# Linear attention and a token and channel mixer: transposes by DMA instead of TensorE

## The chip, the cores and the metric

The kernel runs on one core of a Trainium2 chip. The metric is the device time of one execution in microseconds (us); less is better. A core has TensorE (PE), VectorE (DVE), ScalarE (ACT), GpSimd (POOL) and SyncE (SP), each with its own in-order stream of instructions, and 16 DMA engines that all queues share.

## What is computed

Eight batches, eight heads, 576 tokens, head size 64. The attention's output, heads side by side, is x with 512 columns; the mixer works on it.

```python
q_p, k_p = phi(q), phi(k)            # phi(x) = (x if x > 0 else exp(x) - 1) + 1
kv  = einsum('bhsd,bhse->bhde', k_p, v)
z   = sum(k_p, axis=2)
num = einsum('bhsd,bhde->bhse', q_p, kv)
den = einsum('bhsd,bhd->bhs', q_p, z)[..., None] + 1e-06
x   = (num / den) as [8, 576, 512]
u   = x + (relu(x^T @ w_tok1) @ w_tok2)^T     # w_tok1 576x256, w_tok2 256x576
out = u + relu(u @ w_ch1) @ w_ch2             # w_ch1 512x1536, w_ch2 1536x512
```

Inputs and output are float32 in HBM; the matmuls take bf16 and add up in float32.

## The kernel before

**Tokens.** The first 512 tokens of a batch lie four to a partition (R = 4: token 4p + r is on partition p); the last 64, the tail, lie on one half of the partitions, the lower half for even batches and the upper for odd ones, as a fifth piece r = 4. The tails of a pair of batches share one tile, `ut`, so that the channel part works on pairs: 4 + 4 + 1 tiles of 128 tokens.

**Steps for one batch**, by helper and line. `load` (L98) issues on SP, for one half g of the heads, a 512 KB DMA (L103) and the tail's 64 KB (L107; q's tail goes to both halves of the partitions, two DMAs). `phi` (L137) makes k' into `kp` or q' into `qp`: exp on ACT (L117), +1, min and max on DVE (L123, L131, L132). `vcast` (L142) casts v, with a column of ones per head, so that z comes out of the kv matmul. `kv` (L154): 40 matmuls of 64 columns of weights and 65 moving columns, two heads side by side in the array, copied by ACT into `kvd`, the two heads of a pair on the two halves of the partitions. `qtr` (L181): 20 TensorE transposes of q', copied by ACT (L187) into `qT`. `nd` (L217): 40 matmuls with a contraction of 64, then DVE adds EPS, inverts and multiplies into `x` (L206 to L211), in five pieces. `mm1` (L224) and `mm2` (L237), the token mixer: ten and eight matmuls of 512 columns, relu on ACT (L235), the residual add into `u` on DVE (L245); `mm2_tail` (L248) does the tails of a pair together, in half-width matmuls. `utr` (L258): 16 transposes of u, copied by ACT and DVE into `uT`; `utr_tail` (L330) four for the tails, into `uTt`. `mm3` (L340): four matmuls of 512 columns into one of twelve channel tiles, relu on ACT into `cr` (L350); `mm3_tail` (L352) 16 matmuls of 128 columns. `mm4` (L363): twelve matmuls of 512 columns for one tile of tokens, in three parts, the residual add (L379) and the store (L383), issued on POOL, for the last pair on SP.

**Order.** It is written out by hand. After a start in which batch 0 goes through in small pieces, `run` (L523) takes a list of big steps, `mm3` and `mm4`, and puts small ones behind them at given numbers: "step 10" is what stands behind the eleventh big step. During the big steps of batch n, called stage n in the prediction, the small steps of batch n + 1 run (kv to u), and phi for batch n + 2 (`prep_k` and `prep_q`, L389 and L396), which also issue the loads of the batch after that in the same buffers. An even stage has 24 big steps (12 `mm3`, 12 `mm4`), an odd one 30 (12, 3 of the tail, 15). The numbers are in `at0`, `at1` and `AT` (L554, L573, L583); stage 0 and 1 have lists of their own. Of small steps with one number the one earlier in the list goes first; every engine and the SP queue sees its part of the program in this order. `raw`, `qT`, `x`, `u` and `uT` exist twice, by the parity of the batch; `kp`, `qp`, `vs` and `uTt` once. PSUM has four banks for the big steps and two tiles of two banks, tag "sm", which all small steps take in turn.

**Loads.** Batch 0's are issued first, then the weights; batch 1's, 2's (L504) and 3's (L569) stand between the start and stage 1; from batch 4 on they are issued by `prep_k` and `prep_q` of the batch two earlier.

Of the kernel before, what the change touches and what calls it, by code (L numbers as in the profile page):

```python
# [18 lines left out]
def kernel(  # L19
# [44 lines left out]
    w1t = const("w1t", [128, 128])  # L64
    w2 = const("w2", [128, NT, S])
    wc1 = const("wc1", [128, NDM, DCH])
# [8 lines left out]
    qT = [const(f"qT{b}", [128, HP, R1, 128]) for b in range(2)]  # L75
    kvd = [const(f"kvd{b}", [128, HP, D1]) for b in range(2)]
# [4 lines left out]
    uT = [const(f"uT{b}", [128, NDM, R, 128]) for b in range(2)]  # L81
# [16 lines left out]
    def load(nm, n, g, gate=None):  # L98
        b = n % 2
        hs = slice(HG * g, HG * g + HG)  # L100
        dst = raw[nm, b]
        s = src[nm][n, hs, 0:SM, :].rearrange("h (p r) d -> p h r d", r=R)
        ins = after(nc.sync.dma_start(out=dst[:, hs, 0:R, :].rearrange("p h r d -> p h (r d)"),  # L103
                                      in_=s.rearrange("p h r d -> p h (r d)")), gate)
        for i in range(2):
            if nm == "q" or i == b:
                nc.sync.dma_start(out=dst[half[i], hs, R, :],  # L107
                                  in_=src[nm][n, hs, SM:S, :].transpose([1, 0, 2]))
        return ins
# [44 lines left out]
    def kv(n, g, first=False):  # L154
        b = n % 2
        if first:
            ps = bank()
        else:
            ps = ps_sm.tile([128, 2, 512], FP32, name="kv_ps", tag="sm")[:, 0]
        ps = ps[:, 0:2 * D1].rearrange("p (j e) -> p j e", j=2)  # L160
        for i in range(2):
            for r in range(R1):
                for a in range(2):
                    h = 2 * (2 * g + i) + a
                    nc.tensor.matmul(out=ps[half[a], i], lhsT=kp[:, r, h, :],
                                     rhs=(vst[b] if r == R else vs[:, r])[:, h, :],
                                     start=(r == 0), stop=(r == R))
        nc.scalar.copy(out=kvd[b][:, 2 * g:2 * g + 2], in_=ps)

    def qtr_pair(n, j, tp, put):  # L170
# [5 lines left out]
        if put == "act":  # L176
            nc.scalar.copy(out=qT[b][:, j], in_=tp[:, 0:R1])
        elif put == "dve":
            nc.vector.tensor_copy(out=qT[b][:, j], in_=tp[:, 0:R1])

    def qtr(n, g):  # L181
# [3 lines left out]
        for i in range(2):  # L185
            qtr_pair(n, 2 * g + i, tp[:, i * R1:(i + 1) * R1], None)
        nc.scalar.copy(out=qT[b][:, 2 * g:2 * g + 2].rearrange("p j r c -> p (j r) c"),  # L187
                       in_=tp[:, 0:2 * R1])

    def nd_mm(n, rs, j0, nj):  # L190
        b = n % 2
        ps = ps_sm.tile([128, 2, 512], FP32, name="nd_ps", tag="sm")
        for i, r in enumerate(rs):
            for j in range(nj):
                at = D1 * (nj * i + j)
                for a in range(2):
                    nc.tensor.matmul(out=ps[:, a, at:at + D1], lhsT=qT[b][half[a], j0 + j, r, :],  # L197
                                     rhs=kvd[b][half[a], j0 + j, :], start=True, stop=True)
        live["nd", j0, rs[0]] = ps

    def nd_end(n, rs, j0, nj):
        b = n % 2
        m = nj * len(rs)
        v_ = live["nd", j0, rs[0]][:, :, 0:m * D1].rearrange("p a (i e) -> p a i e", i=m)
        den = work.tile([128, 2, 4], FP32, name="den", tag="den")[:, :, 0:m]
        nc.vector.tensor_scalar(out=den, in0=v_[:, :, :, D:D1].rearrange("p a i o -> p a (i o)"),  # L206
                                scalar1=EPS, scalar2=None, op0=ALU.add)
        nc.vector.reciprocal(out=den, in_=den)  # L208
        for i, r in enumerate(rs):
            js = slice(nj * i, nj * i + nj)  # L210
            nc.vector.tensor_tensor(  # L211
                out=x[b][:, r, 2 * D * j0:2 * D * (j0 + nj)].rearrange(
                    "p (j a d) -> p a j d", j=nj, a=2),
                in0=v_[:, :, js, 0:D],
                in1=den[:, :, js, None].to_broadcast([128, 2, nj, D]), op=ALU.mult)

    def nd(n, r):  # L217
        nd_mm(n, [r], 0, HP)
        nd_end(n, [r], 0, HP)
# [4 lines left out]
    def mm1(n):  # L224
        b = n % 2
        ps = ps_sm.tile([128, NT, DM], FP32, name="a_ps", tag="sm")
        for mt in range(NT):
            for r in range(R):
                nc.tensor.matmul(out=ps[:, mt], lhsT=w1[:, r, 128 * mt:128 * mt + 128],  # L229
                                 rhs=x[b][:, r, :], start=(r == 0), stop=False)  # L230
        for mt in range(NT):
            nc.tensor.matmul(out=ps[:, mt], lhsT=w1t[half[mt]], rhs=x[b][half[mt], R, :],  # L232
                             start=False, stop=True)
# [3 lines left out]
    def mm2(n, rs):  # L237
# [3 lines left out]
        for i, r in enumerate(rs):  # L241
            for kt in range(NT):
                nc.tensor.matmul(out=ps[:, i], lhsT=w2v[:, kt, r], rhs=ar[b][:, kt, :],  # L243
                                 start=(kt == 0), stop=(kt == NT - 1))
        nc.vector.tensor_tensor(out=u[b][:, rs[0]:rs[0] + m], in0=ps[:, 0:m],  # L245
                                in1=x[b][:, rs[0]:rs[0] + m], op=ALU.add)

    def mm2_tail(p):  # L248
        ps = ps_sm.tile([128, 2, DM], FP32, name="h_ps", tag="sm")[:, 0]
        for kt in range(NT):  # L250
            for b in range(2):
                nc.tensor.matmul(out=ps[half[b]], lhsT=w2[:, kt, SM:S], rhs=ar[b][:, kt, :],
                                 start=(kt == 0), stop=(kt == NT - 1))
        for b in range(2):
# [369 lines left out]
```

## Time and profile before

| what | us |
|---|---|
| median of three runs | 306.9 |
| the three runs | 306.6, 307.05, 306.9 |
| the profiled execution | 306.6 |
| its span, first to last instruction | 304.8 |
| PE busy | 278.0 (91%) |
| DVE busy | 165.1 (54%) |
| ACT busy | 159.7 (52%) |
| POOL busy | 26.9 (9%) |
| mean granted TensorE clock | 0.993 of full speed |
| DMA | 42.90 MB, a mean of 141 GB/s |

The page comes from one profiled execution. "Busy" is the time in which an engine works on an instruction; TensorE's matmuls overlap each other, their ends are modelled, and so a row's duration is longer than the distance to the next one. The slices cut the span into 40 parts of 7.62 us; a digit is the busy share in tenths. In a timeline each row has start, duration, engine, line, operation, output and inputs, the number of instructions, and in brackets the idle time before it with what ended it. SPq is the SP queue in the act of issuing a DMA.

### The profile page before, as it was taken

The page shows a single profiled execution, that of the slowest core. Times are in us where ns is not written, and L with a number is a line of the kernel's source. Part 1 is how long each engine was busy: PE and PEld are TensorE (multiplying, and loading weights), DVE is VectorE, ACT ScalarE, POOL GpSimd, SP SyncE. Part 2 cuts the span into 40 slices and gives each one's busy share as a digit, 9 for nine tenths or more (in the row PEclk, how much of TensorE's full clock was granted, in tenths as well). Part 3 has the DMA queues.
Part 4 walks back from the last instruction along what each step waited for, and adds up shares of the span by engine and source line. Part 5 has one row for each costly group of instructions (what it writes and reads, how often), then busy time and mean ns, then how long its engine had stood idle before and what let it go on. Part 6 is the DMA issues. An engine that isn't in the chain of part 4 may idle for free.

```text
span 304.8 us, 5592 instructions
## 1 busy us (share of the span) xinstructions
PE 278.0 (91%) x2274; PEld 146.9 (48%) x2312; DVE 165.1 (54%) x309; ACT 159.7 (52%) x236; POOL 26.9 (9%) x49
## 2 busy tenths in 40 slices
PE   8888969977999999899998999899997999999993
PEld 8765434433744544354464454355463454454641
DVE  4793476395487844981658325791738515440021
ACT  3654753149936476457495075656486074226500
POOL 1070020030001100010001200010000210000000
PEclk9999979999999999999999999999999999999999
DMA  6999998999999920973058710011001210010032
GB/s 196 282 144 205 305 242 201 283 296 338 252 291 290 304 82 0 264 242 117 2 160 243 226 30 0 23 66 53 2 0 37 103 37 0 34 71 34 2 96 76
DMA packets 50585, 42.90 MB, mean 141 GB/s; under 512 B 19136, under 2 KB 47552, under 8 KB 50560
## 3 DMA queue, kind: packets, MB, share of 16 engines
q1 hardware_dynamic: 44064, 31.73, 38.0%
q0 software_dynamic: 6496, 10.82, 14.8%
q8 instruction: 18, 0.29, 0.5%
q14 instruction: 7, 0.06, 0.1%
HBM read 36.83 MB, written 9.44 MB: 152 GB/s over the span
## 4 chain that ended last, share of the span: by engine, by line
PE 57%; DMA 12%; ACT 11%; DVE 8%; SPq 5%; issue 4%; POOL 1%; ACTq 0%
PE h_ps L369 24%; PE c_ps L346 19%; DMA q_raw<-in_q_dram 8%; ACT qT L187 5%; PE a_ps L229 4%; DVE u L245 4%; SPq L107 3%; PE nd_ps L197 3%; DMA wc<-in_moe_w_ch_dram 3%; PE c_ps L357 3%; ACT cr L350 3%; SPq L103 2%; ACT e L117 2%; DVE ut L256 2%; PE tp L266 2%
## 5 line engine op out<-in xcount | busy, mean ns | idle before, releaser
L346 PE MATMUL c_ps<-uT,wc 128*128 128x512 bf16 x366 | 92.0, 380 | 3.7 <-ACT cr L350 1.5
L369 PE MATMUL h_ps<-wc,cr 128*128 128x512 bf16 x371 | 90.6, 383 | 2.2 <-ACT cr L350 1.4
L350 ACT ACTIVATE cr<-c_ps 128x512 bf16<-128x512 f32 x96 | 56.5, 599 | 56.3 <-PE c_ps L346 55.6
L369 PEld LDWEIGHTS <-cr 128*128 128x128 bf16 x384 | 36.1, 99 | 44.3 <-issue 3.5
L346 PEld LDWEIGHTS <-wc 128*128 128x128 bf16 x384 | 33.8, 98 | 39.0 <-issue 5.1
L379 DVE TENSOR_TENSOR o_sb<-h_ps,u 128x512 f32<-128x512 f32 x32 | 21.8, 686 | 20.8 <-PE h_ps L369 20.6
L131 DVE TENSOR_SCALAR e<-e 128x1280 bf16<-128x1280 bf16 (+1 forms) x34 | 16.0, 471 | 30.2 <-ACT e L117 30.2
L383 POOL DMA_DIRECT2D out_dram<-o_sb x24 | 13.8, 576 | 176.8 <-DVE o_sb L379 157.7
L211 DVE TENSOR_TENSOR x<-nd_ps,den 128x512 bf16<-128x512 f32 (+1 forms) x45 | 28.1, 631 | 1.4
L206 DVE TENSOR_SCALAR den<-nd_ps 128x8 f32<-128x8 f32 (+1 forms) x41 | 6.7, 164 | 39.6 <-PE nd_ps L197 37.8
L117 ACT ACTIVATE e<-q_raw 128x1280 bf16<-128x1280 f32 (+1 forms) x18 | 20.3, 1150 | 4.5 <-DMA q_raw<-in_q_dram 3.3
L117 ACT ACTIVATE e<-k_raw 128x1280 bf16<-128x1280 f32 x16 | 20.4, 1273 | 4.0 <-DMA k_raw<-in_k_dram 3.8
L270 ACT COPY uT<-tp 128x1024 bf16<-128x1024 bf16 x7 | 7.1, 1012 | 25.3 <-PE tp L266 25.3
L235 ACT ACTIVATE ar<-a_ps 128x512 bf16<-128x512 f32 x14 | 7.6, 594 | 22.8 <-PE a_ps L232 22.8
L245 DVE TENSOR_TENSOR u<-h_ps,x 128x1024 bf16<-128x1024 f32 x14 | 16.5, 1216 | 5.4 <-PE h_ps L243 5.4
L187 ACT COPY qT<-tp 128x1280 bf16<-128x1280 bf16 x14 | 17.3, 1232 | 1.2 <-PE tp L173 1.2
L123 DVE TENSOR_SCALAR y<-k_raw 128x1280 bf16<-128x1280 f32 x16 | 13.2, 823 | 8.6 <-DMA k_raw<-in_k_dram 8.4
L197 PEld LDWEIGHTS <-qT 64*128 64x128 bf16 x320 | 7.6, 95 | 19.5 <-DVE den L208 8.9
L197 PE MATMUL nd_ps<-kvd,qT 64*128 64x65 bf16 x320 | 13.2, 194 | 3.5 <-ACT qT L187 3.2
L404 PE MATMUL bank<-identity 128*128 128x128 bf16 x178 | 14.0, 247 | 1.4 <-POOL identity masks.py:199 1.4
L145 ACT CAST vs<-v_raw 128x1024 bf16<-128x1024 f32 x14 | 14.9, 1061 | 0.2 <-DMA v_raw<-in_v_dram 0.2
L123 DVE TENSOR_SCALAR y<-q_raw 128x1280 bf16<-128x1280 f32 x16 | 13.3, 829 | 2.3 <-DMA q_raw<-in_q_dram 2.1
(76 smaller groups left out, 263.6 us busy)
## 6 DMA issues: line engine op xcount, KB each, us to landing
k_raw<-in_k_dram SPq DMA_DIRECT2D x16, 512.0 KB, 5.9
q_raw<-in_q_dram SPq DMA_DIRECT2D x16, 512.0 KB, 7.0
v_raw<-in_v_dram SPq DMA_DIRECT2D x16, 512.0 KB, 6.7
out_dram<-o_sb POOLq DMA_DIRECT2D x24, 256.0 KB, 3.9
wc<-in_moe_w_ch_dram POOLq DMA_DIRECT2D x8, 384.0 KB, 8.2
q_raw<-in_q_dram SPq DMA_DIRECT2D x32, 64.0 KB, 6.3
out_dram<-o_sb SPq DMA_DIRECT2D x8, 256.0 KB, 2.4
k_raw<-in_k_dram SPq DMA_DIRECT2D x16, 64.0 KB, 6.0
```

The costliest lines, as they stand in the source:

```text
L117: nc.scalar.activation(out=e, in_=f, func=AF.Exp)
L123: nc.vector.tensor_scalar(out=y, in0=f, scalar1=1.0, scalar2=None, op0=ALU.add)
L131: nc.vector.tensor_scalar(out=e, in0=e, scalar1=1.0, scalar2=None, op0=ALU.min)
L145: copy(out=vs[:, :, hs, 0:D].transpose([0, 2, 1, 3]), in_=raw["v", b][:, hs, 0:R])
L187: nc.scalar.copy(out=qT[b][:, 2 * g:2 * g + 2].rearrange("p j r c -> p (j r) c"), in_=tp[:, 0:2 * R1])
L197: nc.tensor.matmul(out=ps[:, a, at:at + D1], lhsT=qT[b][half[a], j0 + j, r, :], rhs=kvd[b][half[a], j0 + j, :], start=True, stop=True)
L211: nc.vector.tensor_tensor(out=x[b][:, r, 2 * D * j0:2 * D * (j0 + nj)].rearrange("p (j a d) -> p a j d", j=nj, a=2), in0=v_[:, :, js, 0:D] ...
L245: nc.vector.tensor_tensor(out=u[b][:, rs[0]:rs[0] + m], in0=ps[:, 0:m], in1=x[b][:, rs[0]:rs[0] + m], op=ALU.add)
L346: nc.tensor.matmul(out=ps, lhsT=wc1[:, kj, 128 * mc:128 * mc + 128], rhs=uT[b][:, kj].rearrange("p r c -> p (r c)"), start=(kj == 0), stop ...
L350: nc.scalar.activation(out=cr[b][:, mc, :], in_=ps, func=AF.Relu)
L369: nc.tensor.matmul(out=ps, lhsT=crt[:, kc, :] if t == 8 else cr[b][:, kc, 128 * r:128 * r + 128], rhs=wc2[:, kc, :], start=(kc == 0), stop ...
L379: nc.vector.tensor_tensor(out=o, in0=ps, in1=ut[p % 2] if t == 8 else u[b][:, r, :], op=ALU.add)
```

## The change

q and u of batches 2 to 7 are no longer transposed by TensorE through PSUM, but by a DMA, SBUF to SBUF, that goes through the crossbar (`dma_start_transpose`, issued on SP): one for the whole of q' (`qtr_dma`, 128 x 2560 elements), issued by `prep_q` right behind phi, in the stage before that of `nd`; two for u (`utr_dma`, 128 x 1024 each), and one for the tails. Batches 0 and 1 keep TensorE. The layouts of `qT` and `uT` change places of two dimensions to suit this.

kv now takes two heads as 128 columns of weights and 130 moving columns, 20 matmuls; two copies of the diagonal blocks go into `kvbd`, which is zero elsewhere, and `nd` uses it with a contraction of 128 and 130 columns, 20 matmuls in six pieces. q's tail is loaded once, its other half is zero; the tail of the token mixer takes padded weights `w1t` and `w2t` (`w2_tails` fills the latter in stage 0) and runs batch by batch.

The numbers of the small steps change: `nd` begins at 3 instead of 4, `mm2` at 12 instead of 14. The loads of batch 3 stand at step 9 of stage 1 instead of ahead of it, those of batch 4 at step 24 of stage 1 instead of beside phi of batch 2.

```diff
-    w1t = const("w1t", [128, 128])
+    w1t = const("w1t", [128, 2, DTOK])
     w2 = const("w2", [128, NT, S])
+    w2t = const("w2t", [128, NT, 2, 128])
...
-    qT = [const(f"qT{b}", [128, HP, R1, 128]) for b in range(2)]
-    kvd = [const(f"kvd{b}", [128, HP, D1]) for b in range(2)]
+    qT = [const(f"qT{b}", [128, R1, HP, 128]) for b in range(2)]
+    kvbd = [const(f"kvbd{b}", [128, HP, 2 * D1]) for b in range(2)]
...
-    uT = [const(f"uT{b}", [128, NDM, R, 128]) for b in range(2)]
+    uT = [const(f"uT{b}", [128, R, NDM, 128]) for b in range(2)]
...
-        for i in range(2):
-            if nm == "q" or i == b:
-                nc.sync.dma_start(out=dst[half[i], hs, R, :],
-                                  in_=src[nm][n, hs, SM:S, :].transpose([1, 0, 2]))
+        nc.sync.dma_start(out=dst[half[b], hs, R, :],
+                          in_=src[nm][n, hs, SM:S, :].transpose([1, 0, 2]))
...
         for i in range(2):
+            j = 2 * g + i
             for r in range(R1):
-                for a in range(2):
-                    h = 2 * (2 * g + i) + a
-                    nc.tensor.matmul(out=ps[half[a], i], lhsT=kp[:, r, h, :],
-                                     rhs=(vst[b] if r == R else vs[:, r])[:, h, :],
-                                     start=(r == 0), stop=(r == R))
-        nc.scalar.copy(out=kvd[b][:, 2 * g:2 * g + 2], in_=ps)
+                nc.tensor.matmul(out=ps[:, i], lhsT=kp[:, r, 2 * j:2 * j + 2, :],
+                                 rhs=(vst[b] if r == R else vs[:, r])[:, 2 * j:2 * j + 2, :],
+                                 start=(r == 0), stop=(r == R))
+        for i in range(2):
+            nc.scalar.copy(out=kvbd[b][half[i], 2 * g:2 * g + 2, i * D1:(i + 1) * D1],
+                           in_=ps[half[i], :, i * D1:(i + 1) * D1])
...
+    def qtr_dma(n):
+        nc.sync.dma_start_transpose(out=qT[n % 2].rearrange("p r j c -> p (r j) c"),
+                                    in_=qp.rearrange("p r h d -> p (r h d)"))
...
+    def nd_mm(n, g, rs):
         b = n % 2
         ps = ps_sm.tile([128, 2, 512], FP32, name="nd_ps", tag="sm")
         for i, r in enumerate(rs):
-            for j in range(nj):
-                at = D1 * (nj * i + j)
-                for a in range(2):
-                    nc.tensor.matmul(out=ps[:, a, at:at + D1], lhsT=qT[b][half[a], j0 + j, r, :],
-                                     rhs=kvd[b][half[a], j0 + j, :], start=True, stop=True)
-        live["nd", j0, rs[0]] = ps
-
-    def nd_end(n, rs, j0, nj):
-        b = n % 2
-        m = nj * len(rs)
-        v_ = live["nd", j0, rs[0]][:, :, 0:m * D1].rearrange("p a (i e) -> p a i e", i=m)
-        den = work.tile([128, 2, 4], FP32, name="den", tag="den")[:, :, 0:m]
-        nc.vector.tensor_scalar(out=den, in0=v_[:, :, :, D:D1].rearrange("p a i o -> p a (i o)"),
+            for a in range(2):
+                j = 2 * g + a
+                nc.tensor.matmul(out=ps[:, i, a * 2 * D1:(a + 1) * 2 * D1],
+                                 lhsT=qT[b][:, r, j, :], rhs=kvbd[b][:, j, :],
+                                 start=True, stop=True)
+        live["nd", g, rs[0]] = ps
...
+        nc.vector.tensor_tensor(
+            out=x[b][:, rs[0]:rs[0] + m, HG * D * g:HG * D * (g + 1)].rearrange(
+                "p r (h d) -> p r h d", h=HG),
+            in0=v_[:, :, :, 0:D],
+            in1=den[:, :, :, None].to_broadcast([128, m, HG, D]), op=ALU.mult)
...
+            ms = slice(128 * mt, 128 * mt + 128)
+            for r in range(R1):
+                nc.tensor.matmul(out=ps[:, mt], lhsT=w1t[:, b, ms] if r == R else w1[:, r, ms],
+                                 rhs=x[b][:, r, :], start=(r == 0), stop=(r == R))
...
-                                in1=x[b][:, rs[0]:rs[0] + m], op=ALU.add)
-
-    def mm2_tail(p):
-        ps = ps_sm.tile([128, 2, DM], FP32, name="h_ps", tag="sm")[:, 0]
-        for kt in range(NT):
-            for b in range(2):
-                nc.tensor.matmul(out=ps[half[b]], lhsT=w2[:, kt, SM:S], rhs=ar[b][:, kt, :],
-                                 start=(kt == 0), stop=(kt == NT - 1))
-        for b in range(2):
+                nc.tensor.matmul(out=ps[:, i], lhsT=w2t[:, kt, b, :] if r == R else w2v[:, kt, r],
+                                 rhs=ar[b][:, kt, :], start=(kt == 0), stop=(kt == NT - 1))
...
+    def utr_dma(n, rs):
+        b = n % 2
+        nc.sync.dma_start_transpose(
+            out=uT[b][:, rs[0]:rs[0] + len(rs)].rearrange("p r j c -> p (r j) c"),
+            in_=u[b][:, rs[0]:rs[0] + len(rs)].rearrange("p r d -> p (r d)"))
+
+    def utr_tail_dma(p):
+        nc.sync.dma_start_transpose(out=uTt, in_=ut[p % 2])
...
     def prep_k(n, g):
         phi("k", n, HG * g, HG)
         vcast(n, g)
-        if n + 2 < B and n > 1:
+        if n + 2 < B and n > 2:
...
     def prep_q(n, g):
         phi("q", n, HG * g, HG)
-        if n + 2 < B and n > 1:
+        if g == 1:
+            qtr_dma(n)
+        if n + 2 < B and n > 2:
             load("q", n + 2, g)
...
+    def w2_tails():
+        for kt in range(NT):
+            for b in range(2):
+                nc.scalar.copy(out=w2t[:, kt, b, half[b]], in_=w2[:, kt, SM:S])
...
     def steps(n):
 
         out_ = [(f"kv{g}", lambda g=g: kv(n, g)) for g in range(2)]
-        out_ += [(f"qt{g}", lambda g=g: qtr(n, g)) for g in range(2)]
-        out_ += [(f"nd{r}", lambda r=r: nd(n, r)) for r in range(R1)]
+        if n < 2:
+            out_ += [(f"qt{g}", lambda g=g: qtr(n, g)) for g in range(2)]
+        for i, rs in enumerate(([0, 1], [2, 3], [4])):
+            for g in range(2):
+                out_.append((f"nd{i}{g}", lambda g=g, rs=rs: nd(n, g, rs)))
         out_ += [("mm1", lambda: mm1(n)), ("mm2a", lambda: mm2(n, [0, 1])),
-                 ("mm2b", lambda: mm2(n, [2, 3]))]
-        if n % 2:
-            out_.append(("mm2t", lambda: mm2_tail(n // 2)))
-        out_.append(("ut", lambda: utr(n, [0, 1])))
-        if n % 2:
-            out_.append(("utt", lambda: utr_tail(n // 2)))
+                 ("mm2b", lambda: mm2(n, [2, 3])), ("mm2t", lambda: mm2(n, [R]))]
+        if n < 2:
+            out_.append(("ut", lambda: utr(n, [0, 1])))
+            if n % 2:
+                out_.append(("utt", lambda: utr_tail(n // 2)))
+        else:
+            out_ += [("uta", lambda: utr_dma(n, [0, 1])), ("utb", lambda: utr_dma(n, [2, 3]))]
+            if n % 2:
+                out_.append(("utt", lambda: utr_tail_dma(n // 2)))
         return out_
...
-    at0 = {"kv0": 11, "kv1": 11, "qt0": 14, "qt1": 15, "nd0": 16, "nd1": 17, "nd2": 18,
-           "nd3": 19, "nd4": 20, "mm1": 22, "mm2a": 23, "mm2b": 23, "mm2t": 23,
+    at0 = {"kv0": 11, "kv1": 11, "qt0": 14, "qt1": 15, "nd00": 16, "nd01": 17, "nd10": 18,
+           "nd11": 19, "nd20": 20, "nd21": 21, "mm1": 22, "mm2a": 23, "mm2b": 23, "mm2t": 23,
            "ut": 23, "utt": 23}
-    fill = [(5, lambda: phi("k", 1, 0, HG)), (7, lambda: phi("k", 1, HG, HG)),
+    fill = [(0, w2_tails), (2, lambda: mm2(0, [R]))]
...
-    for nm in "kvq":
-        for g in range(2):
-            load(nm, 3, g)
     big = m3(1) + m3t + m4(0, [4, 5, 6, 7, 8])
-    at1 = {"kv0": 10, "kv1": 11, "qt0": 13, "qt1": 14, "nd0": 15, "nd1": 16, "nd2": 17,
-           "nd3": 18, "nd4": 19, "mm1": 21, "mm2a": 24, "mm2b": 25, "mm2t": 26,
-           "ut": 27}
+    at1 = {"kv0": 10, "kv1": 11, "nd00": 13, "nd01": 14, "nd10": 15, "nd11": 16, "nd20": 17,
+           "nd21": 18, "mm1": 20, "mm2a": 22, "mm2b": 23, "mm2t": 25, "uta": 22, "utb": 23}
     fill = [(s, lambda g=g: prep_k(2, g)) for g, s in ((0, 2), (1, 4))]
     fill += [(s, lambda g=g: prep_q(2, g)) for g, s in ((0, 7), (1, 9))]
+    fill += [(s, lambda nm=nm, n=n, g=g: load(nm, n, g)) for n, s in ((3, 9), (4, 24))
+             for nm in "kvq" for g in range(2)]
     fill += [(at1[nm], fn) for nm, fn in steps(2)]
     fill += [(s, lambda g=g: prep_k(3, g)) for g, s in ((0, 20), (1, 22))]
     fill += [(s, lambda g=g: prep_q(3, g)) for g, s in ((0, 26), (1, 28))]
     run(big, sorted(fill, key=lambda e: e[0]))
 
-    AT = {"kv0": 0, "kv1": 1, "qt0": 2, "qt1": 3, "nd0": 4, "nd1": 5, "nd2": 6, "nd3": 7,
-          "nd4": 8, "mm1": 10, "mm2a": 14, "mm2b": 15, "mm2t": 16, "ut": 17, "utt": 19}
+    AT = {"kv0": 0, "kv1": 1, "nd00": 3, "nd01": 4, "nd10": 5, "nd11": 6, "nd20": 7, "nd21": 8,
+          "mm1": 10, "mm2a": 12, "mm2b": 13, "mm2t": 15, "uta": 12, "utb": 13, "utt": 15}
```

## The prediction

> **What bounds the kernel now.** I read the page's slices and chain first, then TensorE's timeline, then the DMA queue's.
>
> ```profile
> PE   8888969977999999899998999899997999999993
> PEclk9999979999999999999999999999999999999999
> DMA  6999998999999920973058710011001210010032
> ...
> PE 57%; DMA 12%; ACT 11%; DVE 8%; SPq 5%; issue 4%; POOL 1%; ACTq 0%
> ```
>
> TensorE is busy nearly everywhere; the DMA engines are full for about 108 us, then idle for long. I call a stage n the run whose channel matmuls are batch n's. By the first L346 matmul of each, stages 1 to 7 begin at 65.05, 102.75, 135.66, 172.85, 205.74, 242.93 and 274.11: lengths 37.7, 32.9, 37.2, 32.9, 37.2, 31.2, 30.7. Inside a stage TensorE's timeline shows what transposes cost:
>
> ```profile
> 80.62 0.72 PE L173 MATMUL tp<-identity,qp 128*128 128x128 bf16 x10
> ...
> 176.53 0.72 PE L173 MATMUL tp<-identity,qp 128*128 128x128 bf16 x10
> 177.09 1.03 PE L346 MATMUL c_ps<-uT,wc 128*128 128x512 bf16 x4
> ...
> 180.19 0.23 PE L197 MATMUL nd_ps<-kvd,qT 64*128 64x65 bf16 x4 [0.48 <-ACT qT L187]
> 180.35 1.04 PE L346 MATMUL c_ps<-uT,wc 128*128 128x512 bf16 x4
> 181.32 0.30 PE L197 MATMUL nd_ps<-kvd,qT 64*128 64x65 bf16 x8
> 181.56 1.04 PE L346 MATMUL c_ps<-uT,wc 128*128 128x512 bf16 x4
> ...
> 197.46 0.62 PE L252 MATMUL h_ps<-ar,w 128*64 128x512 bf16 x4 [0.43 <-DVE u L245]
> ...
> 199.89 0.61 PE L266 MATMUL tp<-identity,u 128*128 128x128 bf16 x8 [0.39 <-DVE ut L256]
> ```
>
> Starts count, as ends are modelled: ten transposes take 0.56 us, four 512-column matmuls 0.865 (0.216 each), and the brackets are stalls. VectorE finishes q of batch 2 at 80.73:
>
> ```profile
> 79.91 0.82 DVE L132 TENSOR_TENSOR qp<-e,y 128x1280 bf16<-128x1280 bf16 x1
> ```
>
> The SP queue and the windows show the loads:
>
> ```profile
> 71.55 0.54 SPq L103 DMA_DIRECT2D q_raw<-in_q_dram  x1
> 72.14 4.25 SPq L107 DMA_DIRECT2D q_raw<-in_q_dram  x2
> ```
>
> ```profile
> 66.30:102.90 36.60, 34.18 (x283) 17.82 (x287) 25.66 (x45) 26.89 (x38) 4.44 (x7) 1.00 1.07 296
> 173.00:205.90 32.90, 30.61 (x235) 14.60 (x238) 20.24 (x36) 19.32 (x28) 2.74 (x5) 1.00 0.12 40
> ```
>
> ```profile
> k_raw<-in_k_dram SPq DMA_DIRECT2D x1, 512.0 KB, 4.7
> ```
>
> A DMA costs SP 0.4 to 0.7 us, more when the engines are full. Stage 1 moves 296 GB/s at a full share (next to last column), stage 4 is empty. The last line, from a window at 154 us, is a 512 KB load on a free queue: 4.7 us to landing, of which 0.52 MB at 300 GB/s is 1.75, so some 2.95 us is fixed.
>
> **What the Trainium skill says.** "DMA: Bandwidth & Descriptors", section "Queues, rings and completion order": on each DMA engine the descriptors of one ring are consumed in order. The trace agrees that SP is held back by what is queued (4.25 us above). The same page, "DMA Transpose (X-bar)", "Constraints": the transpose goes through SP's or ACT's queues, in tiles of 16 partitions by 128 elements; no transpose is in the trace. "TensorE: Matmul & The Clock Gate", Part 1: after an idle window the clock halves for about 3.4 us. The trace agrees: after the wait before 39.94 the granted clock is 0.50 from about 41.5 to 44.7, some 1.6 us lost.
>
> **What it removes.** Per batch from 2 on: q's transposes 2 x 0.56 = 1.12; u's sixteen 0.90 (100.13 to 101.02), and per odd batch the tail's four 0.22. nd: five pieces of 0.34 (the pitch 1.205 less 0.865) = 1.7 become 20 matmuls of 130 columns; at 0.216/512 per column 55 ns each, 1.1. kv: 40 matmuls took 2 x 0.54; 20 twice as wide cost the same. mm1 stays at ten matmuls. The u tail: 0.55 per pair in half-width matmuls becomes 0.43 per batch. So an odd batch frees 1.12 + 0.6 + 0.9 + 0.22 + 0.12 = 3.0, an even one 1.12 + 0.6 + 0.9 - 0.43 = 2.2. The stalls go too: stage 4 has 0.48, 0.43 and 0.39 above and 0.72 for cr at L350, which the earlier mm2a now covers. Ideal lengths: 96 big matmuls 20.8 + fill 6.5 + joints 0.5 = 27.8 in even stages; with 48 tail matmuls 2.7, 12 more big ones 2.6 and a joint, 33.2 in odd ones. Against before: stage 2 saves 5.1, 3 4.0, 4 5.1, 5 4.0, 6 3.4. Stage 1 keeps its 1.5 us wait for ACT and saves 2.2. Stage 0: four q tails of 64 KB fewer before batch 1's q lands (1.0), nd 0.6, half of L256 0.7, about 2.0. The w2 copies, memsets and first mm2 tail lie beside the waits before 42 us: nothing, or 1 us without that cover. Extra kv copies (two of about 0.27) and nd's sixth piece lie on ACT and VectorE, busy 19 and 20 of 32.9 us: nothing; at most 0.2 per stage. ACT loses 2.5 us of qT copies per batch. **Saved: 25.8.**
>
> **What a transpose costs.** Nearest row: the 4.7 us load. The page's table at the end of "Why a DMA increments its semaphore by 16 and not by 1" has 262,144 sequencer cycles for 8,192 tiles (previous generations), 32 a tile; at SP's 1.2 GHz ("Advanced Engine Details and Errata", "Clock Domains") 27 ns. q is 160 such tiles, an estimate of 4.3 us; half of u is 64, 1.7. With the fixed 2.95: **7.2 and 4.65 us.** Below: 261 GB/s ("Latency and other measured facts") gives 2.5 and 1.0, so 5.4 and 3.95. Above: 1309 ns a block ("VectorE: DVE Perf Modes", "The three transpose paths"), 20 blocks serially, 29 us. I take the middle, since one push per tile is described; no gain below zero is possible for a wait.
>
> **Where they wait.** PE is in order, so all matmuls queue behind a late qT or uT. SP is in order too: it now waits for VectorE's q and u, and behind that wait stand only loads for a batch two later, and the last pair's stores.
> - qT(2): q is ready at 80.73, and nd00, now at step 13, is reached at the time of the L173 row, 80.62 (both 2 us earlier). PE waits the whole 7.2, and nd00 starts at 86.0. Seven steps of 0.865 and nd's 1.1 on, step 20 ends at 93.2; nine steps, mm1 2.2, mm2 2.2 and joints 0.5 later the stage's work ends at 105.8.
> - uT(2), end of stage 1. Load 3, formerly issued at 60 to 76 ahead of the stage, now starts after qT(2), near 83, and its 3.5 MB (six pieces of 576 KB) at 300 GB/s end near 96. Loads k, v of batch 5 follow step 20: their 2.4 MB, 8 us, stand around the two halves of u, whose adds end near 99 and 102. SP comes to the second half near 104.4, after four load issues and the first; 4.65 later is 109. Wait 3.2.
> - qT(3). Load 4 moves from steps 2 to 9 (k, v, q beside their phi) to step 24: twelve SP issues, past u(2) and k, v of batch 5; at 26 comes q of batch 5, and only at 28 the transpose. From 107, when u(2) is through: 3.5 + 0.6 MB and two 256 KB stores on POOL's queue, 15.5 us, then the transpose and its landing, 5.5 as part of the push runs ahead: 128. nd00 is due four steps and kv, 4.6, after the stage's start: 113.6. Wait 14.4. SP's twelve issues alone (8 us) would leave half of that.
> - uT(3), end of stage 2: u's second add stands behind the second k phi on VectorE. By stage 4's rows, where mm1 ends at 189.05, that phi's exp ends at 194.3, so the add would end 8.4 after mm1; thirteen steps and mm2, 13.4 after mm1, the stage ends. The loads of batch 6 (from 2.7 on, 7.9 us), both halves (3.4) and landing (2.4) make 16.4. Wait 3.0. qT(4): issued 0.4 after the end, behind 1 us of q's load, so ready at 8.6 and due at 4.6 + 3.0. Wait 1.0.
> - Stage 4 has no loads: uT(5) lands at 8.4 + 4.65 = 13.1, hidden. qT(6) is issued 0.4 after the stage's end and wanted 4.6 after it: 3.0.
> - uT(4), uT(6), uT(7), qT(5), qT(7) and the tails have 5 to 10 us more: nothing; at twice the latency still about nothing.
> Sum 31.8. The two long waits also cost the clock, 1.6 each: 3.2. Otherwise the moved loads are early enough: k of batch 3 lands near 90 and is used at 93, batch 4 ten steps into stage 2; if not, the wait is their lateness, up to 3.
>
> **Sum** against the profiled execution, 306.6 (span 304.8 and 1.8 around it): 306.6 - 25.8 + 31.8 + 3.2 = 315.8. The median of the runs is 0.3 higher: 316.1.
>
> **Rivals.**
> (1) The crossbar is slower, say half the pushing rate: q 11.5, half of u 6.4. qT(2) +4.3, uT(2) +3.4, qT(3) +4.3, uT(3) +3.4, qT(4) +4.3, then uT(5) and qT(6) +5.6: 25.3 more, 341. For it: the spread of prices. Against: the skill's bandwidth row. At the serial price the ring alone would hold 6 x 47 us, and the time pass 400; 0.03 for that.
> (2) The other side: the ring isn't the bound, since transposes pass loads or run at 261 GB/s. The place is stage 2: qT(3) then waits only for SP's issues, 7.4 instead of 14.4; uT(2), uT(3), qT(4) fall by 6.5, qT(2) and qT(6) by 1.8 each: 17.1 less, 299. It decides once all waits stay under 22.6 (25.8 - 3.2). For it: the DMA share is near nothing from 108 to 121 us and after 170. Against: SP's order at step 24.
> (3) Savings and waits cancel: 306.3 to 307.5, within 0.2%, which is about what can be told from no change.
>
> **Numbers.** Forecast 316.1, own range 308 to 326, 0.43; rival 1 0.22 and its extreme 0.03; rival 2 0.27; rival 3 0.05. So slower 0.68, same 0.05, faster 0.27. The range 297 to 345 leaves out some 0.08 below and 0.1 above.
>
> **What would show it.** Right: stage 4 near 28 us with no L173 or L266 rows; a PE wait of about 7 us near 80 and of about 14 some 5 us into stage 2, ended by a DMA into qT; waits of 3 at the starts of stages 2 and 3 for uT. Wrong: qT landing in under 5 us; no wait in stage 2; or rows of tens of us per transpose.

## The result, and the profile after

The changed kernel takes 320.69 us (median of four runs, 319.14 to 320.96), the kernel before 306.75 beside it (306.38 to 307.05): a ratio of 1.0445 (1.0409 to 1.0481), so it is slower by 13.9 us. The profiled execution took 320.51, its span is 318.8. Later runs were on chips where the kernel before took 308.0 to 308.3; they are compared by ratio, and a difference of ratios is turned into microseconds by multiplying with 306.75. (Some executions of a kernel with these transposes are over 1.5% longer than others of the same kernel; the ratios leave them out.)

The page's slices and its chain by engine, for the changed kernel:

```profile
PE   8888989797499270699589999899699999999994
...
PEclk9999999999699876599979999999979999999998
DMA  7999999730996999507990399306700471061022
...
PE 51%; DMA 20%; SPq 9%; DVE 7%; ACT 6%; issue 4%; POOL 1%; ACTq 0%; DVEq 0%
```

Before, TensorE's row had hardly a digit under 8 after the start. Now it has holes at the 11th, 14th, 16th, 17th and 20th slices (8 us each) and a small one at the 29th, with the granted clock low in them or just behind. In the chain, DMA went from 12% to 20% and SP's queue from 5% to 9%, while TensorE fell from 57% to 51%. The list of waits (us in total, times, longest) names who waits for what:

```profile
PE nd_ps L200 <- DMA qT<-qp: 21.0, 4, 11.4
...
PE c_ps L349 <- DMA uT<-u: 11.9, 2, 7.2
```

TensorE's timeline places them (start, length, instruction, and in brackets the wait before it):

```profile
83.58 0.62 PE L200 MATMUL nd_ps<-kvbd,qT 128*128 128x130 bf16 x4 [5.12 <-DMA qT<-qp]
...
112.58 1.86 PE L349 MATMUL c_ps<-uT,wc 128*128 128x512 bf16 x4 [7.22 <-DMA uT<-u]
...
130.24 0.62 PE L200 MATMUL nd_ps<-kvbd,qT 128*128 128x130 bf16 x4 [11.40 <-DMA qT<-qp]
130.65 1.91 PE L349 MATMUL c_ps<-uT,wc 128*128 128x512 bf16 x4
...
160.75 1.87 PE L349 MATMUL c_ps<-uT,wc 128*128 128x512 bf16 x4 [4.72 <-DMA uT<-u]
...
200.91 0.41 PE L200 MATMUL nd_ps<-kvbd,qT 128*128 128x130 bf16 x4 [1.50 <-DMA qT<-qp]
201.16 1.02 PE L349 MATMUL c_ps<-uT,wc 128*128 128x512 bf16 x4
...
231.39 0.41 PE L200 MATMUL nd_ps<-kvbd,qT 128*128 128x130 bf16 x4 [2.98 <-DMA qT<-qp]
231.64 1.78 PE L349 MATMUL c_ps<-uT,wc 128*128 128x512 bf16 x4
```

They are qT(2), uT(2), qT(3), uT(3), qT(5) and qT(6), 32.94 us in sum. Read the first column and the second together: after 11.40 us of waiting, four big matmuls are down for 1.91 instead of 1.02, as the clock is halved; after 1.50 they are at 1.02. Stages 1 to 7 begin at 63.08, 112.58, 160.75, 194.66, 223.66, 261.08 and 288.41, so their lengths are 49.5, 48.2, 33.9, 29.0, 37.4, 27.3 and 30.4. Stages 1 and 2 lost 11.8 and 15.3 us against before; 3, 4 and 6 won 3.3, 3.9 and 3.9.

SP's queue shows why qT(3) is the latest. Its rows from u(2) on, in the changed kernel:

```profile
105.11 1.33 SPq L333 DMA_TRANSPOSE uT<-u  x1
106.49 1.14 SPq L104 DMA_DIRECT2D k_raw<-in_k_dram  x1
...
119.10 1.56 SPq L106 DMA_DIRECT2D q_raw<-in_q_dram  x1
...
121.44 1.06 SPq L106 DMA_DIRECT2D q_raw<-in_q_dram  x1
122.62 5.56 SPq L191 DMA_TRANSPOSE qT<-qp  x1
```

Between u's second half and q's transpose stand batch 4's twelve load issues, 106.49 to 120.66, and q's of batch 5. The transpose is pushed from 122.62 to 128.18, and TensorE goes on at 130.24. The transposes' landing times, in the list of DMA issues (count, median us from issue to landing):

```profile
uT<-u SPq DMA_TRANSPOSE x12, 3.8
qT<-qp SPq DMA_TRANSPOSE x6, 7.2
```

A median hides the spread that matters here: one of q took 5.0 with nothing beside it, and up to 10.3 behind loads; half of u 3.1, and 7.4 and 8.4 for the second halves of u(2) and u(3), behind loads.

### The profile page after: what moved, and what is told of

It reads as the page before. It is cut to its first block, busy times and chain, and to the rows that moved or that the text cites. A ratio compares the mean times of both kernels' runs of the same rounds, so it can differ in the third digit from the quotient of the medians.

```text
span 318.8 us, 4540 instructions
## 1 busy us (share of the span) xinstructions
PE 270.3 (85%) x1744; PEld 148.6 (47%) x1764; DVE 163.6 (51%) x323; ACT 144.6 (45%) x233; POOL 28.8 (9%) x52
## 3 DMA queue, kind: packets, MB, share of 16 engines
q1 hardware_dynamic: 69568, 38.15, 48.2%
## 4 chain that ended last, share of the span: by engine, by line
PE 51%; DMA 20%; SPq 9%; DVE 7%; ACT 6%; issue 4%; POOL 1%; ACTq 0%; DVEq 0%
PE c_ps L349 19%; PE h_ps L372 18%; DMA qT<-qp 9%; SPq L106 5%; PE a_ps L235 5%; DMA q_raw<-in_q_dram 5%; SPq L104 4%; PE nd_ps L200 3%; PE c_ps L360 3%; DMA uT<-u 3%; DMA wc<-in_moe_w_ch_dram 3%; ACT e L116 2%; PE h_ps L246 2%; DVE u L252 2%; DVE y L122 1%
## 5 line engine op out<-in xcount | busy, mean ns | idle before, releaser
L349 PE MATMUL c_ps<-uT,wc 128*128 128x512 bf16 x384 | 97.8, 396 | 14.4 <-DMA uT<-u 11.9
L372 PE MATMUL h_ps<-wc,cr 128*128 128x512 bf16 x374 | 88.6, 381 | 0.7 <-issue 0.2
L349 PEld LDWEIGHTS <-wc 128*128 128x128 bf16 x384 | 37.1, 101 | 52.6 <-issue 20.1
L372 PEld LDWEIGHTS <-cr 128*128 128x128 bf16 x384 | 37.2, 99 | 41.9 <-issue 0.6
L210 DVE TENSOR_SCALAR den<-nd_ps 128x8 f32<-128x8 f32 (+1 forms) x48 | 7.8, 162 | 61.3 <-PE nd_ps L200 60.7
L200 PE MATMUL nd_ps<-kvbd,qT 128*128 128x130 bf16 x160 | 18.5, 237 | 21.5 <-DMA qT<-qp 21.0
L386 POOL DMA_DIRECT2D out_dram<-o_sb x24 | 13.9, 579 | 195.9 <-DVE o_sb L382 170.6
L213 DVE TENSOR_TENSOR x<-nd_ps,den 128x512 bf16<-128x512 f32 (+1 forms) x48 | 28.9, 602 | 1.7
L200 PEld LDWEIGHTS <-qT 128*128 128x128 bf16 x160 | 13.8, 106 | 33.9 <-DMA qT<-qp 22.6
L252 DVE TENSOR_TENSOR u<-h_ps,x 128x1024 bf16<-128x1024 f32 x14 | 17.0, 1218 | 10.3 <-PE h_ps L246 10.3
L116 ACT ACTIVATE e<-k_raw 128x1280 bf16<-128x1280 f32 x16 | 20.3, 1270 | 2.8 <-DMA k_raw<-in_k_dram 2.7
L144 ACT CAST vs<-v_raw 128x1024 bf16<-128x1024 f32 x14 | 14.8, 1056 | 0.1
L122 DVE TENSOR_SCALAR y<-k_raw 128x1280 bf16<-128x1280 f32 x16 | 13.1, 819 | 3.3 <-DMA k_raw<-in_k_dram 3.2
L246 PE MATMUL h_ps<-ar,w 128*128 128x512 bf16 x53 | 14.2, 379 | 0.3
L235 PE MATMUL a_ps<-x,w 128*128 128x512 bf16 x51 | 14.1, 379 | 0.3
```

Of the source, the lines that this page charges most:

```text
L116: nc.scalar.activation(out=e, in_=f, func=AF.Exp)
L122: nc.vector.tensor_scalar(out=y, in0=f, scalar1=1.0, scalar2=None, op0=ALU.add)
L200: nc.tensor.matmul(out=ps[:, i, a * 2 * D1:(a + 1) * 2 * D1], lhsT=qT[b][:, r, j, :], rhs=kvbd[b][:, j, :], start=True, stop=True)
L213: nc.vector.tensor_tensor(out=x[b][:, rs[0]:rs[0] + m, HG * D * g:HG * D * (g + 1)].rearrange("p r (h d) -> p r h d", h=HG), in0=v_[:, :, ...
L235: nc.tensor.matmul(out=ps[:, mt], lhsT=w1t[:, b, ms] if r == R else w1[:, r, ms], rhs=x[b][:, r, :], start=(r == 0), stop=(r == R))
L246: nc.tensor.matmul(out=ps[:, i], lhsT=w2t[:, kt, b, :] if r == R else w2v[:, kt, r], rhs=ar[b][:, kt, :], start=(kt == 0), stop=(kt == NT ...
```

## The experiments

My theory was that of the prediction: the change frees TensorE of some 26 us, and the place of the transposes in SP's ring (the line of transfers that SP has issued and the DMA engines have still to do), behind loads, costs more. The rivals: that the saving itself is smaller and the waits not the cause; that a transpose is slow whatever stands ahead of it; and, once waits were seen to be shared out, that the half clock after them or the step numbers matter as much.

### The saving without the waits

All transposes by DMA write to places that nobody reads; from batch 2 on the matmuls read what batch 1 left. The work of every engine and queue stays.

```diff
-        nc.sync.dma_start_transpose(out=qT[n % 2].rearrange(...
+        nc.sync.dma_start_transpose(out=qT[0].rearrange(...
-                                 lhsT=qT[b][:, r, j, :], rhs=kvbd[b][:, j, :],
+                                 lhsT=qT[1 if n > 1 else b][:, r, j, :], rhs=kvbd[b][:, j, :],
```

and the same for `uT` in `utr_dma` and `mm3`, and for the tail.

> The changed kernel with every DMA, load and step in place, but nobody waits for the new transposes: they are written to the buffers of even parity, while from batch 2 on nd and the channel matmuls read what batch 1 left in the buffers of odd parity (so the output of batches 2 to 7 comes from old q and u). Theory, the loss is PE waiting for landed transposes: the six waits (32.9 us) and the slow clock behind them (about 7) go, 320.7 becomes about 281, 278 to 285. Rival, the removed TensorE work is worth less than I counted, or the wide kv and nd and the tails cost: 295 or more.

Measured: 284.68, ratio 0.925 (0.9214 to 0.9287), so 23.0 us faster than before and 36.7 faster than the change. Undisturbed stages last 27.33 (even) and 32.6 (odd), where the prediction had 27.8 and 33.2. TensorE still waited twice: 1.55 us at 118.0, as late loads of batch 4 had held up ACT, and 3.43 at 132.9. The second comes from VectorE, which can't write the next q' before the transpose of q(3) has read `qp`, the only buffer for it:

```profile
131.41 0.82 DVE L132 TENSOR_TENSOR qp<-e,y 128x1280 bf16<-128x1280 bf16 x1 [6.59 <-DMA qT<-qp]
```

The change's own stalls had covered both. So the saving is real, and what was lost lies in waits for transposes.

### The parts alone

The rest of the change without any DMA transpose: all eight batches through TensorE, loads where they were, the step numbers those of before, but with mm1 one step later (at 11 from stage 2 on), as nd now has six pieces.

```diff
-        if g == 1:
-            qtr_dma(n)
-        if n < 2:
+        if True:
...
-    AT = {"kv0": 0, "kv1": 1, "nd00": 3, "nd01": 4, ... "mm1": 10, "mm2a": 12, ...
+    AT = {"kv0": 0, "kv1": 1, "qt0": 2, "qt1": 3, "nd00": 4, ... "mm1": 11, "mm2a": 14, ...
```

> The rest of the change alone: wide kv and nd, one q tail, padded tail weights; all transposes on TensorE as before and all loads where they were. Theory: stage 0 saves 2, nd 0.6 in each of six batches, the tail of u costs 0.43 in even and saves 0.12 in odd batches: about 302, 300 to 304. Rival, the wide form costs (more ACT copies, another nd piece): 307 or more.

Measured: 292.77, ratio 0.9512 (0.947 to 0.9555). I had expected about 302: this kernel gains 15 us, not 5. Even stages last 29.58, odd ones 34.74. An even stage is 2.25 longer than in the kernel with nobody waiting, which is the sum of q's 1.12, u's 0.90 and the tail's 0.22. The stalls of the kernel before were gone with the transposes still on TensorE.

To find where they went, the kernel before with one number changed:

```diff
-          "nd4": 8, "mm1": 10, "mm2a": 14, "mm2b": 15, "mm2t": 16, "ut": 17, "utt": 19}
+          "nd4": 8, "mm1": 11, "mm2a": 14, "mm2b": 15, "mm2t": 16, "ut": 17, "utt": 19}
```

> The kernel before with mm1 at step 11 instead of 10 from stage 2 on, nothing else. In the kernel with all transposes on TensorE, where mm1 stands at 11, the wait of 0.72 us for cr in even stages is gone. If that is the step number's doing: about 2 us less, 304 to 306. If it is the wide forms': 306 to 308 on the same chip as before.

Measured: 302.06, ratio 0.9791 (0.9754 to 0.9828), 6.4 us for one step, where I had expected about 2. Later stages last 31.3 and 35.6 instead of 32.9 and 37.2; of the stalls that the prediction lists, cr's 0.72 and u's 0.43 are gone and ut's fell from 0.39 to 0.21. ACT's rows of the kernel before show what the step does:

```profile
189.16 1.09 ACT L235 ACTIVATE ar<-a_ps 128x512 bf16<-128x512 f32 x2 [1.46 <-PE a_ps L232]
190.13 1.27 ACT L117 ACTIVATE e<-k_raw 128x1280 bf16<-128x1280 f32 x1
```

At step 10 mm1 stands ahead of k's phi, so ACT idles for mm1, and k's exp, the cast of v and then cr come late. With mm1 at 11 k's exp goes first. Stage 6, which has no phi, lasts 31.18 in both kernels. (The change leaves mm1 at 10, and ACT idles 1.56 there; but its mm2a at 12 gives TensorE work meanwhile, as the prediction said of cr's stall.) TensorE's timeline of the kernel with mm1 at 11 still has the stall for qT:

```profile
178.84 0.24 PE L197 MATMUL nd_ps<-kvd,qT 64*128 64x65 bf16 x4 [0.48 <-ACT qT L187]
```

The other 8.6 us (0.9791 to 0.9512) are left for the wide kv and nd with their new loop order, whose first piece needs only half of q (this stall is gone from batch 3 on), for the tails and for q's single tail load; no run tells these apart.

Then each transpose by itself, all else as in the kernel with TensorE's transposes. u by DMA alone:

> As the kernel with all transposes on TensorE, but u of batches 2 to 7 by DMA; loads where they were before the change. Theory: the sixteen or twenty transposes and the stalls at them go, some 8 us, and waits for u of batches 2 and 3, which stand among loads, come, 5 to 12 with the clock: 298 to 307. Rival, u's transposes are harmless and all loss is q's: about 294.

Measured: 295.91, ratio 0.961 (0.9577 to 0.9644), below the range and nearer to the rival's 294: one wait of 5.98 for uT(2); stages 3 to 6 are 0.9 to 1.1 shorter each than with all on TensorE. What u's transposes free, one wait and its half clock take away, and a little more. q by DMA alone:

> As the kernel with all transposes on TensorE (292.8), but q of batches 2 to 7 by DMA; loads where they were before the change, so the first of these transposes meets a full ring. Theory, a transpose waits for the loads ahead of it: TensorE saves 6 x 1.12 = 6.7, the wait for q of batch 2 grows beyond the 5.1 us that it had with an empty ring, to 8 to 12, others of 2 to 6 follow, with the clock some 23 in all: about 309, 302 to 312. Rival, transposes pass loads: waits no longer than in the changed kernel without load 4, under 300.

Measured: 319.56, ratio 1.0371 (1.0326 to 1.0417), 26.3 us more than all on TensorE. The waits in this kernel:

```profile
PE nd_ps L200 <- DMA qT<-qp: 20.3, 4, 11.4
...
PE h_ps L246 <- DVE u L252: 5.7, 6, 1.6
```

I had expected 309. The waits for qT and the half clock after them come to 26 us (20.3 and 5.8), not 23; less the 6.7 that TensorE saves, q's transposes alone cost some 19, an estimate. The second line most likely comes from my step numbers, not from the transposes: mm1 stands at 10 with mm2a at 14 again, as in the kernel before. With loads in their old place, a q transposed between them is what hurts; u of batch 3 and later has steps to spare.

### The order on SP

Only load 4 goes from step 24 to step 29 of stage 1, behind q(3)'s transpose:

```diff
-    fill += [(s, lambda nm=nm, n=n, g=g: load(nm, n, g)) for n, s in ((3, 9), (4, 24))
+    fill += [(s, lambda nm=nm, n=n, g=g: load(nm, n, g)) for n, s in ((3, 9), (4, 29))
```

> The changed kernel with one number changed: the loads of batch 4 stand at step 29 of stage 1 instead of 24, so behind the transpose of q of batch 3. Theory, the wait of 11.4 us in stage 2 is the SP queue's order: it falls to 2 or less and the one for u of batch 2 (7.2) gets shorter too, as fewer loads are in flight: 306 to 311. Rival, the crossbar is late by itself or the bytes have to be moved anyway: 317 to 321.

Measured: 307.5, ratio 0.9945 (0.9913 to 0.9976), of 20 executions from 303.15 to 314.08; the profiled one took 303.15. SP's queue from the same place:

```profile
104.89 1.32 SPq L333 DMA_TRANSPOSE uT<-u  x1
...
109.28 5.23 SPq L191 DMA_TRANSPOSE qT<-qp  x1
```

The transpose starts 13.3 us sooner, the 11.40 us wait is gone, and the others stay (5.12, 6.67, 5.16, 2.92). 15.3 us for one number: the theory's main term, shown by undoing it.

Next I tried to help u in the same way: load 4 at 29, k and v of batch 5 at 24, those of batches 6 and 7 at step 14, behind u's adds.

> The changed kernel with loads put behind transposes everywhere: batch 4's at step 29, k and v of batch 5 at step 24 of stage 1, those of batches 6 and 7 at step 14 of stages 2 and 3, behind both halves of u. Against the kernel with only batch 4's loads moved (307.5). Theory, the waits for u of batches 2 and 3 (6.7 and 5.2 there) are loads ahead of them on the ring: they fall to 3 or less in sum 4, with less clock lost: 294 to 299. Rival, VectorE's late u and the crossbar's latency set them: 304 to 308.

Measured: 326.02, the four executions from 320.83 to 327.63, against 308.27 for the kernel before. Each is slower than before, where I had expected 294 to 299. The list of waits and the SP queue, of an execution of 326.18, show why:

```profile
PE nd_ps L200 <- DMA qT<-qp: 34.4, 5, 9.9
```

```profile
101.83 4.99 SPq L333 DMA_TRANSPOSE uT<-u  x2
106.91 0.53 SPq L104 DMA_DIRECT2D k_raw<-in_k_dram  x1
...
113.36 1.99 SPq L106 DMA_DIRECT2D q_raw<-in_q_dram  x1
115.46 5.90 SPq L191 DMA_TRANSPOSE qT<-qp  x1
```

The waits for uT fell to 1.92, as the second half of u(2), without loads ahead of it, landed in 3.2 us instead of 7.4. But the loads now stand between u's transposes and q's: batch 5's hold SP from 106.91 on, and q(3) isn't pushed until 115.46. I had looked at which transpose the loads leave and not at which they come to.

So the loads belong where no transpose is about to come, behind q's. All loads of batch n + 1 right behind the transpose of q(n):

```diff
         if g == 1:
             qtr_dma(n)
+            for nm in "kvq" if n + 1 < B else "":
+                for i in range(2):
+                    load(nm, n + 1, i)
```

and the others left out.

> The changed kernel with all loads of a batch, from batch 3 on, issued right behind the transpose of q of the batch before it, so that they run between q's transposes (end of a stage) and u's (its middle), and neither meets loads ahead of it. Theory, both kinds of wait were loads ahead on one ring, and moving them behind u only pushed the wait to q: now only 5.1 for q of batch 2 and some 2 each for u of batch 2 and q of batches 3, 4 and 6 are left, with 3 of clock: 293 to 300. Rival, the transposes are slowed by loads in flight behind them too, or the loads come too late for phi: 305 or more.

Measured: 304.87, ratio 0.9875 (0.9828 to 0.9922): outside the range, at the rival's edge. Waits are 5.11, 1.90, 3.90, 3.52 and 3.61, 18.0 in sum, where about 13 were expected. For u the theory held, its halves landed in 3.1 to 3.7 us; q took 6.4 to 7.2 in five of six, not 5.0. The rival's reason, loads behind a transpose, doesn't fit: q(2) has them right behind it and took 5.0, q(7) has none and took 6.7.

### The clock

Matmuls of the identity with itself, whose result nobody reads, ahead of the five long waits: 80 at step 12 and 115 at 29 of stage 1, 190 and 75 at 2 and 23 of stage 2, 45 at 2 of stage 5, for instance

```diff
+    fill += [(12, lambda: warm(80)), (29, lambda: warm(115))]
```

> The changed kernel with idle-time matmuls of the identity (128 columns, results unused) ahead of its five longest waits, each a little shorter than the wait, so that TensorE keeps its clock. Theory, the waits stay and the 7 us of half clock behind them go: 312 to 316. Rival, the slow clock costs nothing, as the stretches behind the waits are bound by something else: 319 to 322.

Measured: 316.66, ratio 1.0248 (1.0206 to 1.0291), just above the range and 6.0 us less than the change. One row of its windows, where the next to last three columns are granted clock, DMA share and GB/s; after it rows of the change's:

```profile
130.00:136.00 6.00, 6.00 (x44) 3.36 (x43) 5.08 (x17) 3.40 (x6) 0.00 (x0) 1.00 0.06 16
```

```profile
134.00:135.00 1.00, 1.00 (x7) 0.66 (x6) 0.16 (x1) 0.26 (x1) 0.00 (x0) 0.50 0.00 0
201.00:202.00 1.00, 1.00 (x8) 0.55 (x9) 0.57 (x3) 0.00 (x0) 0.00 (x0) 1.00 1.03 349
234.00:235.00 1.00, 1.00 (x4) 0.38 (x3) 0.93 (x3) 0.05 (x1) 0.00 (x0) 0.50 0.00 0
```

In the change the clock is 0.50 nearly four microseconds after qT(3) has landed, and 2.6 after qT(6). From such rows, it stays halved for 4.8, 3.1, 5.9, 2.7 and 3.4 us after the five waits of 2.98 us and more, 19.9 in sum, which is 10.0 us of work lost. The dummies saved only 6.0, since two waits of 2.70 and 2.00 were left after them, each with its halved clock.

### The best use found

TensorE transposes batches 2 and 3 while loads fill the ring, the DMA those from 4 on; nd of odd stages begins at step 8 to give q time.

```diff
-        if g == 1:
+        if g == 1 and n > 3:
-        if n < 2:
+        if n < 4:
```

> TensorE transposes for batches 2 and 3, DMA for 4 to 7, loads as before the change, and in odd stages nd moved to step 8 so that the transpose has 9 us. From the kernel with all on TensorE (292.8): 2.0 less in two stages and 2.2 in two, 8.4, if nothing waits: about 284.5, 283 to 288. Rival, the transposes are late also with a nearly empty ring: 290 or more.

Measured: 290.54, ratio 0.94 (0.9358 to 0.9442), which is the rival's number, with waits of 4.14 for qT(5) and 0.49. SP wasn't late for qT(5): q' was ready at 162.39, and the push began at once,

```profile
162.41 5.44 SPq L191 DMA_TRANSPOSE qT<-qp  x1
```

but it landed after 10.3 us, with the loads of batch 7 and u(4) ahead of it in the ring. With the loads of batches 6 and 7 put behind q's transposes, and nd at step 6:

> As the kernel with DMA transposes from batch 4 on (290.5, with one wait of 4.1 for q of batch 5), but the loads of batches 6 and 7 stand behind the transposes of q of 4 and 5, and nd in odd stages begins at step 6. Theory: that wait and the clock behind it go, 5 to 6: 284 to 287. Rival: 290, if the wait came from SP waiting for u.

Measured: 288.67, ratio 0.9358 (0.9325 to 0.9391), above the 284 to 287 expected. The wait of 4.14 is gone; the interval overlaps with that of the last kernel, so its 1.3 us aren't sure. It has the lowest median of all but the kernel with nobody waiting, and is faster than the kernel before and the change. Its longest wait for q is below; the others are 0.83, 0.55 and 0.28.

```profile
142.50 0.40 PE L200 MATMUL nd_ps<-kvbd,qT 128*128 128x130 bf16 x4 [1.09 <-DMA qT<-qp]
```

Against all on TensorE (0.9512) DMA transposes, put where they hurt least, are worth 4.7 us. As the change has them, they cost 28.6.

## Why the prediction was right, and where its terms were off

The forecast was 316.1, and 320.7 came. The mechanism was right: TensorE is freed of about what was said, and waits for transposes behind loads on SP's ring take more. The runs give this balance, in microseconds:

| term | predicted | measured | from |
|---|---|---|---|
| stalls that mm1 at 11 ends too | | -6.4 | kernel before with mm1 at 11 |
| wide kv and nd, tails, q's tail load | | -8.6 | all on TensorE, less that |
| transposes off TensorE | | -14.8 | nobody waiting: 8.0, and its own waits of 5.0 and their 1.8 of half clock |
| saved, in sum | -25.8 | -29.8 | |
| waits for transposes | 31.8 | 32.9 | TensorE's timeline |
| half clock | 3.2 | 10.0 | granted clock by window |
| sum | +9.2 | +13.1 | +13.9 by the medians |

0.8 us are left over. That the total came so near is partly luck: the saving was larger by 4.0, which hides more than half of the 6.8 by which the half clock was missed, and within the waits 4.0 too little for uT(2) stands against 3.0 too much for qT(3).

**What it saves.** 25.8 was short by 4: pure stages last 27.3 and 32.6, not 27.8 and 33.2 (2.6 over five stages), and stage 1 with nobody waiting 34.5, not 35.5. The list of stalls was right, and so was mm2a as the cover for cr's. But the sentence "The stalls go too" booked them to the change: 6.4 us, cr's and u's above all, go with one step number in the kernel before. Half of the saving (15.0 of 29.8) needs no DMA at all. A sum over a bundle of edits can be right without telling which edit to keep.

**What a transpose costs.** 7.2 us for q is the median that was measured, and this is partly chance. SP's push of q takes 3.17 us, of half of u 1.28, when the ring is free: 20 ns a tile, where the estimate from the Trainium skill ("DMA: Bandwidth & Descriptors", "Why a DMA increments its semaphore by 16 and not by 1") was 27; the measurement decides. Landing after 5.0 and 3.1 us without traffic beside it, it is somewhat below the prediction's lower bounds of 5.4 and 3.95, and the 29 us of the serial price are out. One sign that the prediction named for being wrong, "qT landing in under 5 us", was all but met, with the time near the forecast all the same. The transpose was quicker than taken, and the ring mattered more.

**The waits, one by one.** qT(2): 5.1 for 7.2, the free landing. uT(2): 7.2 for 3.2. SP was to come to the second half near 104.4, and came at 105.11; the stage's work was to end at 105.8, and ended at 105.36. The term that failed is "4.65 later is 109": it landed 7.4 after its push, with four load issues of batch 5 between it and the first half; with those loads moved behind it, it landed in 3.2. qT(3): 11.4 for 14.4. It landed at 130.2, not 128, but stage 2 began at 112.6, not 109, and at half clock reached nd00 6.3 us into the stage, not 4.6. uT(3): 4.7 for 3.0, again a second half behind loads (8.4 to landing). qT(4) and qT(5): none and 1.5, for 1.0 and none. qT(6): 2.98 for 3.0. The errors nearly cancel.

**The half clock** is the term most off: 10.0 for 3.2. "The two long waits also cost the clock, 1.6 each" counted two of five, and took each at the 1.6 of one earlier example; the shorter waits of 2.98 to 5.12 us cost 1.4 to 2.4 each, and the longest 3.0.

**The rivals.** The slower crossbar (341) is out by its landing times. The ring that isn't the bound (299) had the better rate and still lost: it needed all waits under 22.6, and they are 32.9, because of SP's order at step 24, the very point it named against itself. Moving load 4 by five steps gives 20.1 of waits and 305.1 by ratio, so that rival's turning point is about where it was put.

**What stays open.** Why q lands in 6 to 7 us late in the kernel, and in 5.0 for q(2), wasn't tested by itself. In the change q(7) has no load near it and took 6.8. In those 6.8 us SP's queue moves the transpose (first line: packets, MB, share of 16 engines) and POOL's the stores of `out` (second):

```profile
q1 hardware_dynamic: 2592, 0.66, 55.1%
q0 software_dynamic: 207, 0.65, 29.0%
```

The stores take 29.0% of 6.8, 2.0 us of the engines' time, about what q(7) took longer than q(2), 1.8. That they are the cause is an estimate; no run moved them. Nor did a run issue the transposes on another engine's queue than the one with the loads.

## What to carry to other kernels

A transpose given to the DMA costs its place in a ring: list all that the queue's engine issues between the data being ready and the transpose, and put loads behind the transpose that has little time, not ahead of it. Where a change comes as a bundle, run its parts alone: here the rest, with mm1 a step later, was worth 15 us, and the headline cost 28.6. Price a wait on TensorE with the clock that it may cost afterwards: here 1.4 to 3.0 us more after most waits of 2 us and above, not only after the longest.

## What the runs showed of the hardware

- A transpose from SBUF to SBUF goes out in small packets. The page's packets under 512 B rose from 19,136 to 44,512. In the window of q(2)'s transpose alone, below, a DMA share of 0.72 of 5.2 us is 3.7 us of all 16 engines, for 2,560 rows or 160 packets each: 23 ns a packet of 256 B. So 0.66 MB takes the engines as long as 1.1 MB of loads at 300 GB/s.

```profile
78.40:83.60 5.20, 0.08 (x3) 0.03 (x2) 0.00 (x0) 1.60 (x5) 0.00 (x0) 0.80 0.72 131
```

- The length of a wait alone doesn't decide whether the clock is halved after it. Over the traces of all runs, the clock stayed full after waits for transposes of 1.43 to 1.92 us and was halved after every one of 3.61 us and more, 18 in number. Between these it did both: halved after 2.00, 2.68, 2.70, 2.94 and 2.98 us, full after 2.03, 2.92 and 3.52. The half clock ended 2.7 to 6.0 us after TensorE went on, and not later after longer waits in any regular way: in the change, 3.1 after 7.22 us, 4.8 after 5.12.
